# A decode kernel's last weight matrix loaded in two pieces instead of five, with seven tiny loads behind it

## The chip, the cores and the metric

The kernel runs on one core of one Trainium2 chip. The metric is device time in microseconds, the median of several executions. Beside it stands one profiled execution, with a trace of every engine and every DMA packet.

## The reference

One token (a row `x` of 1024 values, bf16) goes through an attention block with a key and value cache and, beside it, an MLP mixer; both are added to `x`. Cut to what matters here:

```python
xn = layernorm(x)
# A: 32 query heads over 4 groups of keys and values, 65536 keys of 128 values each
q = xn @ wq
p = softmax(q @ k.T * 128**-0.5);  o = p @ v;  a = o @ wo
# B: S is 1, so shifting along the sequence leaves zeros
h   = gelu(layernorm(xn) @ w1);   hs = shifted(h) @ w2;   x1 = xn + hs
b   = x1 + gelu(layernorm(x1) @ w3) @ w4          # w3: 1024 x 3584, w4: 3584 x 1024
out = x + a + b
```

With one token, `shifted(h)` is zero and `x1` is `xn`, but the kernel still loads `w1` and `w2` and multiplies by them. The caches are 64 MB for the keys and 64 MB for the values (in units of 1024 x 1024 bytes); every weight is read once. So the work is some 170 MB of reads with little arithmetic on each byte.

## The kernel before, in words

All large operands go through five buffers (`SLOTS`, line 16) of 32 KB in each of 128 partitions. A list, `items` (lines 82 to 91), gives the order in which they are loaded and used: the two halves of `wq`; then for each of four groups four times a tile of 16384 keys (K) and one of values (V), with `w3` and `w1` put in between; `wo` for the group after its tiles; at the end `w2` and the pieces of `w4`. `issue` (line 98) takes a slot and starts one DMA for one item on SP's queue (line 118). The loop at line 440 calls `ensure(i + LOOKAHEAD)`, which issues items up to four ahead, and then computes item `i`. A load waits on SP until the slot that it takes, that of the item five places before, has been read.

A K tile is transposed in place by VectorE (line 353), multiplied by the queries on TensorE (line 357), and its scores go through a maximum (line 361), an exponential on ScalarE (line 374) and a transpose (line 377); the V tile is multiplied by the result (line 389). `group_end` (line 399) joins the four tiles of a group.

The output row is accumulated in one PSUM tile, `psB`, by `row_acc` (line 159, the matmul is line 160): row 0 holds columns 0 to 511 and row 32 columns 512 to 1023, in two column groups of TensorE. A vector of one column is the stationary operand, and 512 columns of a weight row block are streamed through. `compute_wo` does 16 such matmuls for each group, `compute_w2` 16.

`w4` has 3584 rows, 28 for each partition. A "row" of a piece, in what follows, means one of these 28: 128 rows of the matrix, one in each partition, 256 KB in all, and two matmuls (columns 0 to 511 and 512 to 1023). `W4_PIECES` (line 19) says how many of them each load of `w4` has: 16, 8, 2, 1 and 1. `compute_w4(q)` (line 326) does 2 matmuls for each row of piece `q`, once that piece has landed. Its vector, `dst_h`, was made far earlier by `compute_w3`. After the last piece ScalarE copies one half of `psB` (line 336) and issues its store (line 339), and VectorE copies the other half (line 337), which SP stores (line 340).

The layout of `w4` puts the 28 rows of a partition one behind the other in memory, 2 KB each; a piece of n rows is n x 2 KB in a stretch for each partition:

```python
w4_v = B_w4.rearrange("(m c) n -> m c n", c=FC)
c0 = w4_start[item[1]]
src = w4_v[:, c0:c0 + W4_PIECES[item[1]], :].rearrange("p c n -> p (c n)")
```

Each DMA on the queues of SP and ScalarE is given one of eight semaphores in turn (they are called lanes below); a DMA that takes a lane waits until the lane's DMA before it has landed. At the end of the kernel all have to have landed.

## Time and profile before

| | |
|---|---|
| median of 3 executions | 406.71 us (406.63 to 406.77) |
| the profiled execution's own time | 406.69 us |
| its span, first to last instruction | 404.8 us |
| TensorE matmuls, busy | 245.7 us (61%) |
| VectorE, busy | 215.7 us (53%) |
| ScalarE, busy | 37.7 us (9%) |
| bytes moved by DMA | 170.11 MB, 420 GB/s over the span |
| mean granted TensorE clock | 0.796 of full |

The page of the profile gives busy times, a row of slices in time, the DMA queues, and the chain of work that ended last, followed back from the end. Lines of the timeline give start and length in microseconds, the engine (PE is TensorE, PEld its weight loads, DVE VectorE, ACT ScalarE, SPq the sequencer of SP that issues DMAs), the line of the kernel, the operation with output and inputs, and in brackets the idle time before it and what ended it. Views of stretches give the busy time of each engine in a window, the number of instructions that were at work in it, the clock that TensorE was granted, the mean share of the 16 DMA engines that was busy, and GB/s. Views of DMA issues give the size of each load and the time from issue to landing.

### The profile page before, as it was taken

The page shows a single profiled execution, that of the slowest core. Times are in us where ns is not written, and L with a number is a line of the kernel's source. Part 1 is how long each engine was busy: PE and PEld are TensorE (multiplying, and loading weights), DVE is VectorE, ACT ScalarE, POOL GpSimd, SP SyncE. Part 2 cuts the span into 40 slices and gives each one's busy share as a digit, 9 for nine tenths or more (in the row PEclk, how much of TensorE's full clock was granted, in tenths as well). Part 3 has the DMA queues.
Part 4 walks back from the last instruction along what each step waited for, and adds up shares of the span by engine and source line. Part 5 has one row for each costly group of instructions (what it writes and reads, how often), then busy time and mean ns, then how long its engine had stood idle before and what let it go on. Part 6 is the DMA issues. An engine that isn't in the chain of part 4 may idle for free.

```text
span 404.8 us, 3326 instructions
## 1 busy us (share of the span) xinstructions
PE 245.7 (61%) x1400; PEld 95.7 (24%) x1400; DVE 215.7 (53%) x235; ACT 37.7 (9%) x60; POOL 11.2 (3%) x30
## 2 busy tenths in 40 slices
PE   0385565328475847557657948384659474758456
PEld 0132222103132312112223313131233121213122
DVE  0419474017484848346665847475748383838500
ACT  0101101100201010120210010101010101010100
POOL 5001000000000000000010000000000000000000
PEclk9998878857795778768595868888958797679898
DMA  8999999999999999999999999999999999999993
GB/s 363 415 424 449 418 426 434 430 418 444 434 408 439 447 416 419 458 418 416 447 431 413 437 444 414 435 440 418 430 440 424 428 439 427 425 437 413 440 415 134
DMA packets 7065, 170.11 MB, mean 420 GB/s; under 512 B 1023, under 2 KB 1033, under 8 KB 1418
## 3 DMA queue, kind: packets, MB, share of 16 engines
q1 hardware_dynamic: 6772, 169.87, 98.0%
q8 instruction: 11, 0.18, 0.2%
q0 software_dynamic: 128, 0.02, 0.0%
q10 hardware_dynamic: 150, 0.01, 0.0%
q14 instruction: 4, 0.03, 0.0%
HBM read 169.88 MB, written 0.01 MB: 420 GB/s over the span
## 4 chain that ended last, share of the span: by engine, by line
DMA 54%; PE 23%; DVE 17%; ACT 2%; another core or an unknown queue 1%; issue 1%; DVEq 0%; ACTq 0%
DMA slot<-in_A_k_cache_dram 44%; DVE slot L353 11%; PE sc L357 10%; DMA slot<-in_B_w_dram 7%; PE psB L160 5%; PE oacc L389 4%; DMA x_bf<-in_A_x_dram 3%; DVE pT L377 2%; DVE mx L361 2%; ACT p_sb L374 2%; PE rows L244 1%; PE pm_e L417 1%; DVE m L365 0%; PE pm_mx L363 0%
## 5 line engine op out<-in xcount | busy, mean ns | idle before, releaser
L353 DVE STREAM_TRANSPOSE slot<-slot 128x2048 f32<-128x2048 f32 x64 | 142.3, 2281 | 61.1 <-DMA slot<-in_A_k_cache_dram 61.1
L357 PE MATMUL sc<-slot,qst 128*128 128x512 bf16 x512 | 131.6, 411 | 40.9 <-DVE slot L353 40.9
L389 PE MATMUL oacc<-slot,pT 128*32 128x512 bf16 x512 | 56.0, 616 | 48.0 <-DVE pT L377 48.0
L357 PEld LDWEIGHTS <-qst 128*128 128x128 bf16 x512 | 51.6, 103 | 125.1 <-issue 45.9
L361 DVE TENSOR_REDUCE mx<-sc 128x1 f32<-128x1024 f32 x16 | 19.6, 1225 | 34.7 <-PE sc L357 34.7
L374 ACT ACTIVATE p_sb<-sc,nball 128x1024 bf16<-128x1024 f32 x16 | 17.8, 1114 | 209.8 <-DVE nball L372 209.8
L389 PEld LDWEIGHTS <-pT 128*32 128x32 bf16 x512 | 17.5, 139 | 75.0 <-DVE pT L377 49.4
L377 DVE STREAM_TRANSPOSE pT<-p_sb 128x1024 bf16<-128x1024 bf16 x16 | 19.9, 1245 | 23.3 <-ACT p_sb L374 23.3
L244 PE MATMUL rows<-slot,xpad 128*32 128x512 bf16 (+1 forms) x144 | 13.6, 509 | 6.1 <-DMA slot<-in_B_w_dram 6.1
L363 PE MATMUL pm_mx<-ident_f,mx 128*1 128x128 f32 x16 | 4.3, 270 | 21.1 <-DVE mx L361 21.1
L160 PE MATMUL psB<-slot,oT 128*1 128x512 bf16 x64 | 12.6, 564 | 4.3 <-DVE oT L428 4.3
L394 ACT COPY ob<-oacc 128x512 f32<-128x512 f32 x12 | 7.0, 586 | 58.6 <-PE oacc L389 58.6
L160 PE MATMUL psB<-slot,dst_h 128*1 128x512 bf16 x56 | 7.9, 444 | 3.2 <-DMA slot<-in_B_w_dram 3.2
L370 PE MATMUL pm_mx<-ident_f,rep 1*128 1x1 f32 x16 | 3.5, 222 | 9.9 <-DVE rep L367 9.9
L417 PE MATMUL pm_e<-og,selbig 128*128 128x128 f32 x32 | 7.4, 403 | 3.4 <-DVE og L409 3.4
L244 PEld LDWEIGHTS <-xpad 128*32 128x32 bf16 x144 | 5.7, 127 | 15.0 <-issue 13.7
L172 PE MATMUL pm_ln<-ln_rowsum_a,ones_f 128*128 128x1 f32 x2 | 0.6, 348 | 13.6 <-DVE psel L229 13.6
L337 DVE CAST out<-psB 64x256 bf16<-64x256 f32 x1 | 0.4, 417 | 15.2 <-ACT out L336 15.2
L363 PEld LDWEIGHTS pm_mx<-ident_f,mx 128*1 128x1 f32 x16 | 1.3, 79 | 29.0 <-DVE mx L361 29.0
L417 PEld LDWEIGHTS pm_e<-og,selbig 128*128 128x128 f32 x32 | 6.3, 293 | 6.7 <-DVE og L409 6.7
L365 DVE TENSOR_REDUCE m<-pm_mx 1x8 f32<-1x128 f32 x16 | 4.4, 278 | 5.8 <-PE pm_mx L363 5.8
L374 ACT ACT_TABLE_LOAD x3 | 3.8, 1283 | 35.6 <-DVE nball L372 35.6
(97 smaller groups left out, 79.3 us busy)
## 6 DMA issues: line engine op xcount, KB each, us to landing
slot<-in_A_k_cache_dram SPq DMA_DIRECT2D x16, 4096.0 KB, 34.5
slot<-in_A_v_cache_dram SPq DMA_DIRECT2D x16, 4096.0 KB, 35.5
slot<-in_A_wq_dram SPq DMA_DIRECT2D x2, 4096.0 KB, 21.4
slot<-in_A_wo_dram SPq DMA_DIRECT2D x4, 2048.0 KB, 38.4
slot<-in_B_w_dram SPq DMA_DIRECT2D x2, 3584.0 KB, 42.6
slot<-in_B_w_dram SPq DMA_DIRECT2D x3, 2048.0 KB, 26.9
slot<-in_B_w_dram SPq DMA_DIRECT2D x1, 4096.0 KB, 27.8
slot<-in_B_w_dram SPq DMA_DIRECT2D x1, 512.0 KB, 16.1
```

The costliest lines, as they stand in the source:

```text
L160: nc.tensor.matmul(psB[32 * j:32 * j + 1, :], lhsT=lhsT, rhs=rhs, start=(not row_started[j]), stop=False, tile_position=(0, 32 * j), skip_ ...
L244: nc.tensor.matmul(acc[32 * j:32 * j + 32, bk, 0:width], lhsT=xp[:, c, :], rhs=wt[:, cl, ch * width:(ch + 1) * width], start=(c == 0), sto ...
L353: nc.vector.transpose(out=kf[:, cg, :], in_=kf[:, cg, :])
L357: nc.tensor.matmul(sc[:, hf, :], lhsT=qst[g % 2][:, o:o + 128], rhs=kr[:, cg, hf, :, bp // 2, :, bp % 2], start=(cg == 0 and bp == 0), sto ...
L361: nc.vector.reduce_max(out=mx[:], in_=sc[:].rearrange("p h n -> p (h n)"), axis=AX.X)
L363: nc.tensor.transpose(pm[0:1, 0:P], mx[:, 0:1], ident_f[:])
L365: nc.vector.reduce_max(out=m8[:], in_=pm[0:1, 0:P].rearrange("o (j h) -> o h j", h=8), axis=AX.X)
L374: nc.scalar.activation(out=p_sb[:], in_=sc[:], func=ACTF.Exp, bias=nball[:, r:r + 1], scale=SCALE, accum_out=lall[:, r:r + 1])
L377: nc.vector.transpose(out=pT[:], in_=p_sb[:])
L389: nc.tensor.matmul(oacc[32 * u:32 * (u + 1), :], lhsT=pT[:, hf, 32 * t:32 * (t + 1)], rhs=vt[:, :, hf, t, :], start=(hf == 0 and t < 4), s ...
L394: nc.scalar.copy(out=ob[:], in_=oacc[:])
L417: nc.tensor.matmul(pe[:, 0:P], lhsT=selbig[:, cg, :], rhs=og[:, 128 * cg:128 * (cg + 1)], start=(cg == 0), stop=(cg == 3))
```

## The change

`w4` comes in two loads, of 16 and of 12 rows, instead of five. As soon as the last load has been issued, seven loads are issued on the same queue, from the first bytes of `x` into a small tile that nothing reads: 8 bytes for each of 9, 10, 11, 12, 13, 14 and 15 partitions. They take lanes like all other loads; in the order of SP's instructions the fourth to seventh wait for the landing of the last V tile, of `wo` of the last group, of `w2` and of the first piece of `w4`, and SP's store of the output, behind them, waits for the landing of the first of them. On the other engines the instructions and their order are the same; only the waits of the `w4` matmuls are fewer. The added lines shift later line numbers: 118 becomes 119, 160 becomes 161, 340 becomes 341.

```diff
-W4_PIECES = (16, 8, 2, 1, 1)
+PROBES = (9, 10, 11, 12, 13, 14, 15)
+W4_PIECES = (16, 12)
...
+
+    probe = const.tile([16, 16, 4], BF16, name="probe")
+    xv = A_x[0, 0, :].rearrange("(p c) -> p c", c=32)
+    probed = False
     for i, it in enumerate(items):
         ensure(i + LOOKAHEAD)
+        if n_issued[0] == len(items) and not probed:
+            probed = True
+            for k in PROBES:
+                nc.sync.dma_start(out=probe[0:k, k - 1, :], in_=xv[0:k, 0:4])
         compute[it[0]](*it[1:])
```

## The prediction

> **What bounds the kernel now.** I read the page first, its slices in time and its queues. Nearly all bytes come through one queue, SP's, and the DMA engines are full in every slice but the last. (First row: DMA share in tenths over 40 slices of 10.1 us; second: packets, MB, share of the time of 16 engines.)

> ```profile
> DMA  8999999999999999999999999999999999999993
> ...
> q1 hardware_dynamic: 6772, 169.87, 98.0%
> ```

> So up to some 395 us the time is bytes over bandwidth, and the change moves no byte there. What is left to change is the last slice. I therefore read the end of the chain of waits (start us, length us):

> ```profile
> 365.42 27.79 DMA slot<-in_B_w_dram
> 393.21 0.04 issue
> 393.26 7.49 PE psB L160 x54
> 400.75 0.01 issue
> 400.76 0.40 PE psB L160 x2
> ```

> The wait for w4's first piece ends at 393.21; TensorE then works 28 rows of two matmuls with one short stop, and ends at 401.15. The copies and stores of the output end the span at 404.8. The profiled execution took 406.69 us, 1.89 more than its span, and the median of the runs is 406.71; I add differences to 406.69.

> Next the DMA issues of this stretch (KB, us from issue to landing), with issue times from SP's timeline: 374.86, 383.30 (374.86 + 8.77 - 0.33), 388.38, 390.11.

> ```profile
> slot<-in_B_w_dram SPq DMA_DIRECT2D x1, 2048.0 KB, 23.3
> slot<-in_B_w_dram SPq DMA_DIRECT2D x1, 512.0 KB, 16.1
> slot<-in_B_w_dram SPq DMA_DIRECT2D x1, 256.0 KB, 11.7
> ...
> slot<-in_B_w_dram SPq DMA_DIRECT2D x1, 256.0 KB, 10.6
> ```

> Issue plus landing time gives the arrivals of w4's pieces: 16 rows 393.22, 8 rows 398.16, 2 rows 399.40, 1 row 400.08, 1 row 400.71. The early arrivals of small pieces are what the kernel lives from: when the last byte lands, one row is left to multiply.

> What a row costs is in TensorE's timeline (start, length, then the weight loads, which go with the rows):

> ```profile
> 386.45 1.89 PE L160 MATMUL psB<-slot,oT 128*1 128x512 bf16 x16 [1.06 <-DVE oT L428]
> ...
> 395.34 0.13 PEld L160 LDWEIGHTS <-dst_h 128*1 128x1 bf16 x2 [0.29 <-issue]
> 395.77 0.13 PEld L160 LDWEIGHTS <-dst_h 128*1 128x1 bf16 x2 [0.29 <-issue]
> ```

> At full granted clock 16 matmuls are 8 rows in 1.89 us; the last matmul lasts 0.38 (median 379 ns at this line), so a row takes (1.89 - 0.38)/7 = 0.2155 us. At half clock rows start 0.427 us apart (395.34, 395.77), and a matmul lasts 0.63 (the longest at this line).

> **The change, part by part.** *Three loads go (2, 1 and 1 rows); the 8-row load becomes one of 12.* Bytes are the same. Nothing starves by that: the queue holds the 4 MB piece and more when the 12-row load is issued at 374.86, so only the order of issue changes. The 12-row piece has landed when all its 3 MB have: 398.16 plus 1 MB. In before that MB took 2.55 us (400.71 - 398.16) in small packets; in big ones 2 MB took 4.94 (398.16 - 393.22), so 2.47 a MB. The packet view shows at most more: from 366 to 390 us 10.21 MB at 99.5% of 16 engines, 26.7 KB per engine-us; from 396.5 to 400.4 us 0.65 MB at 44.4%, 23.5; by that ratio 2.55 becomes 2.24. I take 400.63, with bounds 400.40 and 400.71.

> *TensorE's last 12 rows move behind that landing.* In before, 11 of them ran beside the arrivals from 398.2 on; that cover goes. Start 400.63 + 0.04 = 400.67. At full clock 11 x 0.2155 + 0.38 = 2.75, so TensorE ends at 403.42 instead of 401.15: **+2.27**. Everything after (ScalarE's and VectorE's copies, two stores) follows unchanged.

> *The clock of these 12 rows.* The gap before them is new: the 16 rows of the first piece end near 398.37 (393.26 + 8 rows at 0.427 less 0.19 for the first and eighth step, + 8 at 0.2155 + 0.165), so TensorE stands still for 2.3 us; where those rows run at full clock it is 3.8 us (from 396.87). The granted clock changes in this trace only on a grid of 3.41 us. One call for such stretches (stretch, length, TensorE busy us, ..., granted clock, DMA share, GB/s):

> ```profile
> 188.12:191.53 3.41, 1.51 (x7) 0.46 (x5) 1.72 (x3) 0.00 (x0) 0.00 (x0) 1.00 0.96 413
> 191.53:194.94 3.41, 0.26 (x1) 0.18 (x1) 0.47 (x2) 2.49 (x3) 0.00 (x0) 0.50 0.94 404
> 280.28:283.69 3.41, 1.65 (x11) 0.74 (x8) 3.41 (x2) 0.59 (x1) 0.00 (x0) 1.00 0.96 413
> 283.69:287.10 3.41, 2.82 (x13) 1.07 (x12) 3.41 (x3) 0.00 (x0) 0.00 (x0) 1.00 0.98 416
> 297.34:300.76 3.42, 2.56 (x25) 0.85 (x18) 1.34 (x2) 0.00 (x0) 0.00 (x0) 0.50 0.99 422
> 300.76:304.17 3.41, 2.34 (x12) 2.04 (x14) 0.94 (x4) 0.00 (x0) 0.00 (x0) 0.50 0.96 413
> 379.26:382.68 3.42, 2.60 (x28) 0.99 (x32) 2.67 (x6) 0.00 (x0) 0.00 (x0) 0.50 1.13 484
> 382.68:386.09 3.41, 1.85 (x22) 1.27 (x14) 1.41 (x4) 0.00 (x0) 0.00 (x0) 1.00 0.98 423
> ```

> The reader is to see two thresholds. From full clock, 1.51 of 3.41 us busy (44%) is followed by half and 1.65 (48%) by full. From half clock, 2.56 (75%) stays half and 2.60 (76%) rises. Half clock thus lasts at least one whole stretch, in which 3.41/0.427 = 8 rows pass, at 8 x (0.427 - 0.2155) = 1.69 more than at full clock. Which of three ends comes depends on where the grid lies:
> - *All full.* On the grid of this execution the stretch 396.33 to 399.74 is busy for 2.04 us (60%), so the next one is full, to 403.16: +2.27.
> - *One half stretch.* Grid 1.09 later (397.42, 400.84, 404.25): busy 1.14 before the gap and 0.17 behind it is 38%, so half clock from 400.84; 8 rows pass until 404.25, the rest at full: +2.27 + 1.69 = **+3.96**. Where the half stretch reaches past the tail it is less, down to about +3.4.
> - *All half.* Grid 0.13 earlier, where the first piece runs at full clock and ends at 396.87: 396.20 to 399.61 is busy 20%, so half from 399.61; the next stretch is busy 2.35 of 3.41 (69%, below 75%), so it stays half: 400.67 + 11 x 0.427 + 0.63 = 406.00: +4.85.

> Working the two thresholds through the tail at 25 equally spaced positions of the grid, with the landings above, gives about 3 times the first, 15 times the second and 7 times the third. Nothing in one profile shows whether the grid lies alike in every execution; the 0.14 us spread of before says nothing, as its end hangs on the landing at 400.71 and not on the clock.

> [...]

> *The seven probes.* In the order of SP's instructions in the changed program they follow the last w4 load. Each issue is 0.33 us (the rows of SP's timeline), 7 x 0.33 = 2.3 us, less three removed; SP is idle from 390.4 to 402.0 in before. The fourth to seventh wait for the landings of the last V, wo, w2 and w4's first piece, the latest at 393.22; behind them stands only SP's output store, ready at 402.02 in before and later now. That store also waits for the landing of the first probe, which is queued right behind the 12 rows. Bounds: nothing, or a small load's 6.9 us (dst_g, 2 KB) counted from 400.63: 407.5, which is 1.6 past the store's new time of 405.98 (402.02 + 3.96). The nearest row is w4's last piece, also small and queued behind others: it landed 0.63 after its neighbour, so 401.3 for the probe, well in time. I take nothing. The last probe, issued at 393.3, would at the 12.3 us of x_bf land at 405.6, before the end of the span in any case.

> [...]

> **The rivals.**
> - *All full clock*, 406.69 + 2.27 = 408.96. For it: the grid of the one profile. Against: few grids.
> - *All half*, 406.69 + 4.85 = 411.54. For it: 7 of 25 positions.
> - *Not slower*: the engines' shares after 396.5 us (0.63 over 2.5 us, 0.10 over 2.2 us) show that engines finish one by one. If one big load let them end together, the last landing would be 396.5 + 1.58 + 0.22 = 398.3, as the first piece's rows end; 398.35 + 2.75 = 401.10, so 406.65. From a landing of 398.3 down the change costs nothing, and above 399.2 it costs over 0.2% (0.81 us, about what a measurement can tell from no change). Against: the 8 rows alone landed at 398.16 with 1 MB to come, and nothing moves bytes between engines.
> - *The probes hold the end* (or a load of nine to fifteen partitions is slow in a way no row shows): 410.65 + 1.6 = 412.25.

> **How the numbers follow.** One half stretch 0.52 (410.65, own range 410.0 to 410.8), all full 0.20, all half 0.18, probes 0.06, not slower 0.04 (half of it faster, half the same). Forecast 410.65. The range takes in all full with the early landing (408.73) up to all half with the late one (411.62): 408.7 to 411.7, 0.90 of the chance; without its lower end it would hold 0.70. Slower 0.96, same 0.02, faster 0.02.

> **What would show it.** The 12-row load lands at 400.4 to 400.7; TensorE waits there once, for a w4 DMA, and starts 24 matmuls right after; its end is 2.75 us later with clock 1.00, 4.4 with one half stretch, 5.3 with all half. The clock's grid lies elsewhere than here. Times of single runs differ by more than the 0.14 us of before, if the grid is free. Wrong would be: a landing before 399.2, a first probe that lands after the output copies, or a half clock that a gap of 2.3 us doesn't bring.

## The result, and the profile after

The changed kernel took 409.45 us (median of 3 executions, 409.40 to 410.89), before 406.71. The ratio is 1.0081, with a 95% interval of 1.0059 to 1.0103: slower by 0.8%. The profiled execution took 409.45 us with a span of 407.7.

The page of the changed kernel, slices and queue as they were shown of before. (DMA share in tenths; SP's queue with packets, MB, share of 16 engines.)

```profile
DMA  8999999999999999999999999999999999999990
...
q1 hardware_dynamic: 6508, 169.87, 97.2%
```

The same bytes in 264 packets fewer, and the last slice, a 3 in before, is now a 0: the loads are over, and TensorE still works. The end of its chain of waits (start us, length us, what):

```profile
372.36 1.91 PE sc L358 x8
374.27 0.02 issue
374.28 25.61 DMA slot<-in_B_w_dram
399.89 0.04 issue
399.94 4.33 PE psB L161 x24
404.26 0.02 issue
404.29 0.37 ACT out L337
```

In before the last landing, at 400.71, was followed by 2 matmuls. Here the last landing comes at 399.89 and is followed by 24, that is by all 12 rows. The timeline of TensorE says how they went (start, length, then weight loads, which go with the rows):

```profile
392.65 3.62 PE L161 MATMUL psB<-slot,dst_h 128*1 128x512 bf16 x32 [1.28 <-DMA slot<-in_B_w_dram]
399.94 4.30 PE L161 MATMUL psB<-slot,dst_h 128*1 128x512 bf16 x24 [3.67 <-DMA slot<-in_B_w_dram]
...
400.74 0.13 PEld L161 LDWEIGHTS <-dst_h 128*1 128x1 bf16 x2 [0.29 <-issue]
401.17 0.13 PEld L161 LDWEIGHTS <-dst_h 128*1 128x1 bf16 x2 [0.30 <-issue]
```

The 16 rows ran at full clock (3.62 us, rows 0.2155 apart). The 12 rows start 3.67 us later, at first 0.43 apart (400.74, 401.17): half clock. The view of stretches, on this execution's grid of 3.41 us (stretch, length, TensorE busy us, ..., granted clock, DMA share, GB/s):

```profile
382.63:386.05 3.42, 1.58 (x18) 1.19 (x10) 1.65 (x5) 0.00 (x0) 0.00 (x0) 1.00 1.00 431
386.05:389.46 3.41, 3.32 (x16) 0.99 (x18) 0.03 (x1) 0.00 (x0) 0.00 (x0) 0.50 0.98 420
...
396.29:399.70 3.41, 0.00 (x0) 0.00 (x0) 0.00 (x0) 0.00 (x0) 0.00 (x0) 1.00 0.29 106
399.70:403.11 3.41, 3.17 (x16) 1.00 (x17) 0.00 (x0) 0.00 (x0) 0.00 (x0) 0.50 0.00 0
403.11:406.53 3.42, 1.13 (x10) 0.26 (x6) 0.42 (x1) 0.37 (x1) 0.00 (x0) 1.00 0.00 1
```

The new gap filled the stretch before 399.70 (busy 0.00), the next stretch had half clock, and the rows that were left then ran at full. The first two lines show the same thing earlier: a stretch busy for 1.58 of 3.41 us (46%) was followed by half.

### The profile page after: what moved, and what is told of

Read it like the earlier page. It is cut to its first block, busy times and chain, and to the rows that moved or that the text cites. A ratio compares the mean times of both kernels' runs of the same rounds, so it can differ in the third digit from the quotient of the medians.

```text
span 407.7 us, 3328 instructions
## 1 busy us (share of the span) xinstructions
PE 244.4 (60%) x1400; PEld 94.3 (23%) x1400; DVE 215.7 (53%) x235; ACT 37.7 (9%) x60; POOL 11.2 (3%) x30
## 2 busy tenths in 40 slices
DMA packets 6801, 170.11 MB, mean 417 GB/s; under 512 B 1143, under 2 KB 1153, under 8 KB 1154
## 3 DMA queue, kind: packets, MB, share of 16 engines
q1 hardware_dynamic: 6508, 169.87, 97.2%
## 4 chain that ended last, share of the span: by engine, by line
DMA 61%; PE 18%; DVE 16%; ACT 2%; another core or an unknown queue 1%; issue 1%; DVEq 0%; ACTq 0%
DMA slot<-in_A_k_cache_dram 52%; DVE slot L354 11%; PE sc L358 11%; DMA slot<-in_B_w_dram 6%; DMA x_bf<-in_A_x_dram 3%; PE oacc L390 2%; PE psB L161 2%; PE rows L245 1%; DVE pT L378 1%; DVE mx L362 1%; ACT p_sb L375 1%; ACT L184 0%; DVE m L366 0%; PE pm_e L418 0%
## 5 line engine op out<-in xcount | busy, mean ns | idle before, releaser
L378 DVE STREAM_TRANSPOSE pT<-p_sb 128x1024 bf16<-128x1024 bf16 x16 | 19.9, 1245 | 23.3 <-ACT p_sb L375 23.3
L418 PE MATMUL pm_e<-og,selbig 128*128 128x128 f32 x32 | 6.5, 364 | 3.4 <-DVE og L410 3.4
## 6 DMA issues: line engine op xcount, KB each, us to landing
slot<-in_A_wo_dram SPq DMA_DIRECT2D x4, 2048.0 KB
slot<-in_B_w_dram SPq DMA_DIRECT2D x2, 2048.0 KB
```

Source lines behind the costliest of these rows:

```text
L378: nc.vector.transpose(out=pT[:], in_=p_sb[:])
L418: nc.tensor.matmul(pe[:, 0:P], lhsT=selbig[:, cg, :], rhs=og[:, 128 * cg:128 * (cg + 1)], start=(cg == 0), stop=(cg == 3))
```

## The experiments

Each kernel was timed in turn with before on one chip; where a time of before is given here, it is the one measured beside the kernel. Experiments 9 to 12 come from what the first eight left open. The edits of 1 to 7 are shown against the changed kernel, those of 9 to 12 against before.

**1. The tiny loads taken away** (label e1_no_probes).

```diff
-PROBES = (9, 10, 11, 12, 13, 14, 15)
+PROBES = ()
```

> The two big pieces without the seven tiny loads. Theory (the 12 rows of work behind the last landing, part of them at half clock, are the whole cost): as the changed kernel, 409.4 to 410.9, with single runs that differ by over 1 us. Rival (the tiny loads hold the output store or the end): back to about 406.7, or at least 1.5 below the changed kernel.

Measured: 409.49 (six executions: 407.99, 409.16, 409.33, 409.64, 409.69, 410.57), before 406.57, ratio 1.0068 (1.0054 to 1.0083). The tiny loads are not the cost. The six times lie in three places, one near 408.0, four from 409.2 to 409.7, one at 410.6; the changed kernel's three lie at the second and third. The profiled execution was the first, and its chain and stretches show why it was quick:

```profile
374.12 25.89 DMA slot<-in_B_w_dram
400.01 0.04 issue
400.05 2.77 PE psB L161 x24
```

```profile
394.94:398.35 3.41, 1.43 (x14) 0.49 (x11) 0.00 (x0) 0.00 (x0) 0.00 (x0) 1.00 0.62 257
398.35:401.77 3.42, 1.72 (x16) 0.70 (x17) 0.00 (x0) 0.00 (x0) 0.00 (x0) 1.00 0.05 22
```

The same gap of 3.7 us and the same landing (400.01 beside 399.89), but the grid lies 2.1 us later, the gap is shared by two stretches that are busy 42% and 50%, and both are followed by full clock. The 12 rows take 2.77 us instead of 4.33. That 42% is below the 44% after which, in before's trace, the clock fell; the lower threshold is not as sharp as the prediction had it.

**2. The tiny loads alone, behind the old five pieces** (label e2_probes_only).

```diff
-W4_PIECES = (16, 12)
+W4_PIECES = (16, 8, 2, 1, 1)
```

> The old five pieces with the seven tiny loads behind them. Theory: 406.7, within 0.2 us of before, since the last tiny load lands about 1.3 us behind the last piece and the output store comes later than that. Rival (the tiny loads cost): 408 to 409.5.

Measured: 406.12 (405.92 to 406.44), before 406.57, ratio 0.9989 (0.9981 to 0.9998). The tiny loads don't cost, but neither theory had it 0.45 us faster. Experiments 8 to 11 come back to that.

**3. TensorE kept at work in the gap** (label e3_busy_gap).

```diff
+        if q == 0:
+            junk = ps_M.tile([P, 512], F32, name="pm_junk", tag="pm")
+            for cl in range(10):
+                for j in range(2):
+                    nc.tensor.matmul(junk[32 * j:32 * j + 1, :], lhsT=st["hT"][:, cl:cl + 1],
+                                     rhs=wt[:, cl, 512 * j:512 * (j + 1)], start=True, stop=True,
+                                     tile_position=(0, 32 * j), skip_group_check=True)
         if q == len(W4_PIECES) - 1:
```

> The changed kernel with 20 more matmuls (ten rows' worth, into a tile that nothing reads) between the 16 rows and the 12, so that TensorE works through most of the gap. Theory (half clock in the tail costs 1.5 to 1.7 us of the change): all 12 rows at full granted clock, 2.75 us from landing to end instead of 4.3, so 407.9, and single runs within 0.4 us of one another. Rival (the rows cost the same whatever stands before them): 409.4 or more.

Measured: 408.01 (407.94 to 408.08), before 406.57, ratio 1.0035 (1.0023 to 1.0047). More work, less time: 1.5 us below experiment 1, and the spread of 2.6 us is gone (0.14). TensorE's timeline, with the added matmuls at line 338:

```profile
392.81 3.62 PE L161 MATMUL psB<-slot,dst_h 128*1 128x512 bf16 x32 [1.50 <-DMA slot<-in_B_w_dram]
396.26 2.33 PE L338 MATMUL pm_junk<-slot,dst_h 128*1 128x512 bf16 x20
400.11 2.75 PE L161 MATMUL psB<-slot,dst_h 128*1 128x512 bf16 x24 [1.53 <-DMA slot<-in_B_w_dram]
```

The 12 rows take 2.75 us, as worked out for full clock. So of the changed kernel's cost half clock is 1.5 us in the median.

**4. One row of the 12 multiplied** (label e5_one_row); 11 rows of `w4` are left out of the product.

```diff
-        for cl in range(n):
+        for cl in range(n if q == 0 else 1):
```

> The changed kernel with only one of the 12 rows multiplied (11 rows of w4 are left out of the product, the loads are the same). It times the landing of the big piece by itself. Theory (fewer and bigger packets save 0.1 to 0.3 us, the rest of the 0.82 us by which the profiled landing was earlier is chance): 406.4 to 406.6. Rival (the big piece itself lands 0.8 us earlier): 405.9. Second rival (a landing that is late in most runs): above 406.8.

Measured: 405.76 (405.45 to 406.08), before 406.57, ratio 0.9978 (0.9969 to 0.9987). The big piece landed at 400.05, so the first rival had the number right: the landing is earlier than before's as a rule (0.5 to 0.7 us here), not by chance. Its cause is another matter: experiment 9 gives most of it to where the buffers lie. With the clock as granted, the work of 11 rows is worth 409.49 - 405.76 = 3.7 us.

**5. Four rows last** (label e4_last_four), without tiny loads.

```diff
-W4_PIECES = (16, 12)
+W4_PIECES = (16, 8, 4)
```

> Pieces of 16, 8 and 4 rows, no tiny loads: four rows instead of 12 behind the last landing, and no gap of more than about 1 us before them. Theory: from the landing to TensorE's end 0.04 + 3 x 0.2155 + 0.38 = 1.07 us at full clock, against 0.44 in before; with packets a little bigger 407.0 to 407.2, single runs within 0.6 us of one another. Rival (a wait before the last piece brings half clock whatever its length): 4 rows at half clock, 1.95 us, so 408.

Measured: 406.61 (406.48 to 406.92), before 406.57, ratio 1.0002 (0.9993 to 1.0011). The time is 0.4 us below the lower end of what was expected. The tail itself is as worked out (landing 400.03, the 8 matmuls 1.03 us at full clock, gap 0.55 us), but it starts 0.5 to 0.7 us earlier than in the two profiles of before (400.54 and 400.71), which hides it. Behind this gap of 0.55 us the clock stayed full.

**6. Seventy tiny loads** (label e6_seventy).

```diff
-PROBES = (9, 10, 11, 12, 13, 14, 15)
+PROBES = (9, 10, 11, 12, 13, 14, 15) * 10
```

> The changed kernel with ten times its tiny loads, 70 instead of 7. The profiled changed kernel shows their landings 0.2 us apart behind the big piece. Theory (that spacing is a cost of each tiny load, hidden only as long as they are few): the last of 70 lands about 14 us after the big piece, at 414, and the end with it: 415 to 417. Rival (the cost is the packets' own 9 ns, and the spacing is something else): 409.4 to 410.9 as with seven.

Measured: 429.92 (2 executions), before 406.57. Both expectations missed. SP's timeline shows the price, and SP's waits from 374 to 430 us (total, times, longest) tell what it is:

```profile
400.25 25.32 SPq L450 DMA_DIRECT2D probe<-in_A_x_dram  x63
425.62 0.60 SPq L341 DMA_DIRECT2D out_dram<-out  x1
...
SPq L450 <- DMA probe<-in_A_x_dram: 7.0, 1, 7.0
SPq L450 <- DMA out_dram<-out: 0.9, 1, 0.9
```

The eighth tiny load waits until the first has landed, behind the big piece; that is the one long wait, 7.0 us, and it ends at 400.2. Then SP issues the other 63 in 25.32 us, 0.40 each, and on the way waits only once, for 0.9 us. So the price is SP's own time for issuing a load (the prediction had 0.33 us for each), not a wait for lanes. The last tiny load of experiment 2 landed 1.4 us after its issue, so with eight lanes, as an estimate, the waits alone would let one go every 0.2 us. The output store stands behind all of them on SP. With seven there is no such queue: in the changed kernel SP issued the last of them at 392.6 and waited for the first to land until 400.0, 5.1 us before the store was due.

**7. The pieces of 2 and 1 rows as one of 3** (label e7_four_pieces), without tiny loads.

```diff
-W4_PIECES = (16, 12)
+W4_PIECES = (16, 8, 3, 1)
```

> Pieces of 16, 8, 3 and 1 rows, no tiny loads: as before, but the pieces of 2 and 1 rows are one. TensorE ends the 8 rows 0.7 us before the last landing and the 3 rows just at it, so one row is left, as in before. Theory: the landing decides, one load fewer saves less than 0.1 us: 406.4 to 406.6 beside a before of 406.57. Rival (the last landing of before is late by itself, by the 0.5 us that the kernels of the first set show): 406.0 to 406.2.

Measured: 406.17 (405.91 to 406.34), before 406.57, ratio 0.9989 (0.9980 to 0.9998). Again 0.4 below before, with nearly before's pieces.

**8. Before once more** (label r_before), unchanged.

> The kernel before, unchanged, profiled once more. In the first set the old pieces with tiny loads ran at 406.12 and before at 406.57, and w4's first landing was 0.4 to 0.7 us earlier in the five profiles after the first. Theory (the earlier landings come with other programs, not with the tiny loads or the sizes): first w4 landing at 393.1 to 393.3 again, 406.6. Rival (the one profile of before was a late one by chance): 392.6, and a time as its other runs.

Measured: 406.54, first `w4` landing 393.02, last 400.54. Before's landings are no accident; in the eight other kernels so far they were 0.2 to 0.7 us earlier from the first `w4` piece on, ahead of any byte that the change concerns. What those kernels share is the small tile `probe`, which I had left allocated even where nothing was loaded into it. In the compiled programs it moves what is allocated behind it, the five big buffers among it, by 128 bytes per partition: they begin at byte 37856 of a partition in before and at 37984 in the changed kernel.

**9. That tile alone** (label f1_pad128), in before.

```diff
+    pad = const.tile([P, 64], BF16, name="pad")
     for i, it in enumerate(items):
```

> The kernel before with a tile of 128 bytes per partition that nothing uses, allocated where the changed kernel has its small tile; it moves the five big buffers 128 bytes up (37856 to 37984 bytes from the partition's start). Theory (the 0.4 us by which the first set's kernels had w4 earlier come from where the buffers lie): 406.15, first w4 landing near 392.6. Rival (they come from something else in those programs): 406.55.

Measured: 406.09 (405.96 to 406.63), before 406.51, ratio 0.9990 (0.9981 to 0.9999). A tile that nothing touches gives the 0.4 us, as in experiments 2 and 7. Experiments 2 and 9 differ by 0.03 us, less than their runs scatter, so no cost of the seven tiny loads can be told from none. In the profile, of an execution of 406.23, `w4` landed first at 392.93, later than the 392.6 that was expected and 0.1 to 0.3 earlier than in before.

**10. 32 bytes instead** (label f2_pad32): the buffers begin at 37888, 148 times 256.

```diff
+    pad = const.tile([P, 16], BF16, name="pad")
     for i, it in enumerate(items):
```

> The kernel before with 32 bytes put there instead, so that the buffers begin at 37888, a multiple of 512. Theory (what counts is the place in a block of 256 or 512 bytes): at least as early as with 128 bytes, 406.0 to 406.15. Rival (any move does it, or none): the same time as with 128 bytes, whichever that is.

Measured: 404.55 (404.42 to 404.79), before 406.51, ratio 0.9951 (0.9939 to 0.9962). This beats before and the changed kernel, by more than either expectation had. The stream itself is faster; the packet views of the stretch from 100 to 300 us, in which the loads never stop, for before, for the 128 bytes and for the 32 bytes:

```profile
DMA packets 3302, 86.06 MB, mean 430 GB/s; under 512 B 414, under 2 KB 416, under 8 KB 416
```

```profile
DMA packets 3303, 86.10 MB, mean 430 GB/s; under 512 B 414, under 2 KB 416, under 8 KB 416
```

```profile
DMA packets 3312, 86.39 MB, mean 432 GB/s; under 512 B 414, under 2 KB 416, under 8 KB 416
```

A packet is 0.03 MB, and before profiled again has 86.00, so this view tells the 32 bytes from the rest but not the 128 bytes from none. The records of the packets do. A packet of 32 KB took on average, from 60 to 350 us, 1219.5 and 1219.9 ns in the two profiles of before, 1218.8 with the 128 bytes and 1214.4 with the 32 bytes; the changed kernel has 1218.7. As an estimate, each of the 16 engines handles some 324 such packets (170.11 MB), so 5.1 ns a packet make 1.7 of the 2.0 us, and 0.7 to 1.1 ns make 0.2 to 0.4 of the 0.4 us. VectorE's transposes in the same buffers last 2.28 us in all of these kernels, so it is not the compute on the buffers that changed.

**11. Two pieces and nothing else** (label f3_two_pieces_only), before with `W4_PIECES = (16, 12)`, buffers where before has them.

```diff
-W4_PIECES = (16, 8, 2, 1, 1)
+W4_PIECES = (16, 12)
```

> The kernel before with pieces of 16 and 12 rows and nothing else: no tiny loads and no small tile, so the buffers lie as in before. Theory: the two pieces cost 2.5 to 4.5 us in single runs by where the clock's grid lies, and the place of the buffers takes back 0.4 in the changed kernel; so 409.8 here, single runs over 1 us apart. Rival (the small tile's 128 bytes do nothing): 409.4 as the changed kernel.

Measured: 409.88 (408.52, 409.70, 409.77, 409.99, 410.05, 410.89), before 406.51, ratio 1.0080 (1.0066 to 1.0093). This is the cost of the pieces with nothing given back: +3.4, beside +2.7 to +2.9 with the small tile. The profiled execution has the short gap of the prediction's main case (16 rows partly at half clock, 2.01 us idle):

```profile
394.38:397.79 3.41, 3.41 (x20) 1.09 (x18) 0.00 (x0) 0.00 (x0) 0.00 (x0) 0.50 0.84 358
397.79:401.21 3.42, 1.41 (x14) 0.50 (x12) 0.00 (x0) 0.00 (x0) 0.00 (x0) 1.00 0.11 43
401.21:404.62 3.41, 3.41 (x18) 0.95 (x14) 0.00 (x0) 0.00 (x0) 0.00 (x0) 0.50 0.00 0
```

A stretch that is busy for 1.41 of 3.41 us (41%), with a gap far shorter than itself, was followed by half clock.

**12. 288 bytes** (label f4_pad288): the buffers begin at 38144, 149 times 256, no multiple of 512.

```diff
+    pad = const.tile([P, 144], BF16, name="pad")
     for i, it in enumerate(items):
```

> The kernel before with 288 bytes put there, so that the big buffers begin at 38144, a multiple of 256 and not of 512. Theory (blocks of 256 bytes are what counts): 404.55 as with 32 bytes. Rival (blocks of 512 bytes, or the first multiple only by chance): 406.1 or more.

Measured: 404.52 (404.39 to 404.70), before 406.54, ratio 0.9950 (0.9937 to 0.9964). The start at 149 times 256 gives the same time as that at 148 times 256 (404.55), so the gain doesn't hang on a multiple of 512. The packet view from 100 to 300 us:

```profile
DMA packets 3316, 86.52 MB, mean 433 GB/s; under 512 B 414, under 2 KB 416, under 8 KB 416
```

A packet of 32 KB took 1214.4 ns again.

## Why the prediction was right, and where it was not

The sign, the mechanism and the range held: 12 rows wait for the last landing, alone, and part of them run at half clock. The likeliest case was put at 410.65, 1.20 too high. In the profiled execution the terms are these.

- **Landing of the last piece: 400.63 said, 399.89 measured, -0.74.** This is the term that was mis-sized, outside its own bounds (400.40 to 400.71). The part of it that I argued, big packets, was roughly right: from the first piece's landing the last 3 MB took 7.28 us (392.61 to 399.89) beside 7.50 in before, so -0.22 where I took -0.08; experiment 11, which has nothing but the two pieces, shows 7.31, and before profiled again 7.52. The rest was there before: the first piece landed 0.60 earlier, some 0.4 of it from the place of the buffers (by the times of experiment 9), 0.2 within what two profiles of before differ by (393.21 and 393.02). I had taken the small tile for nothing but a target of tiny loads.
- **The 12 rows: landing to TensorE's end 4.48 said, 4.37 measured.** At full clock 2.79 was said; experiment 1's profile has 2.81 and experiment 3's 2.82.
- **From TensorE's end to the time: 5.54 in before, 5.19 after, -0.35.** The prediction had everything after the rows unchanged. Of it some 0.2 lies between TensorE's end and the span's end (3.65 and 3.44, with spans to 0.1 us); all profiled kernels with two pieces show 3.37 to 3.44 there, the others 3.62 to 3.74, but for the seventy loads, whose store is held up. What makes it, the runs don't tell.
- **Half clock: +1.69 said, +1.5 in the median** (409.49 in experiment 1 less 408.01 in experiment 3). The three cases appear as three groups of times in experiments 1 and 11 together: 2, 8 and 2 of 12 executions, where 25 positions of the grid had given 3, 15 and 7. Two of the groups are each tied to a profile; the highest is put to the all-half case by its time alone. Right in kind, wrong in two details. On this execution's grid, 0.04 us from that of before, I had all rows at full clock. `wo`'s rows had run at half clock here (46% busy in the stretch before). So they ended later, `w2`'s rows fell into the next stretch and kept it busy, the 16 rows ran at full clock where in before they had begun at half, and the gap became a whole idle stretch. So the position of the grid alone doesn't decide. The other detail is the lower threshold, which is taken up below the list.
- **Whether the grid is free** was open. The grids of the profiled executions, counted from the span's start, lie from 0.02 to 3.02 us past a multiple of 3.41, and those of before's two profiles are 2.6 us apart; it is free. With TensorE kept at work the two-piece kernel's scatter went from 2.6 to 0.14 us (experiment 3), so it comes from the clock of the 12 rows; before scatters by 0.6.
- **The probes: nothing said, and nothing that can be told from the scatter measured** (experiments 2 and 9).
- **Not slower**: it needed a landing of 398.3; the landings of the big piece were 399.89 to 400.33. The traces have 16 landing records for each of these loads: those of the changed kernel's big piece lie from 396.56 to 399.89, over 3.33 us, and those of the last load in before from 397.35 to 400.71, over 3.36 us, so one big load didn't let its parts end together. It was rightly small.

Before's trace put the lower threshold between 44 and 48% of a stretch, and other profiles don't bear that out. After full clock, a stretch busy for 42% was followed by full in experiment 1, and one busy for 52% by half in experiment 5:

```profile
382.32:385.73 3.41, 1.78 (x22) 1.19 (x10) 1.46 (x4) 0.00 (x0) 0.00 (x0) 1.00 0.96 413
385.73:389.14 3.41, 3.11 (x16) 1.00 (x18) 0.23 (x1) 0.00 (x0) 0.00 (x0) 0.50 0.95 408
```

So from about 41% to over 50% the busy share alone doesn't tell what follows, and what else decides stays open; the counts of 3, 15 and 7 rest on a threshold that isn't sharp. The upper one is sharper: in all fourteen profiles stretches up to 77% stayed at half, and those from 76% rose.

## What to carry to other kernels

When a load-bound kernel ends on a matrix product, the work that is left after the last landing is the cost; size the last pieces so that one piece's work fits into the next one's transfer, and no more than that: a last piece of 4 rows cost 0.4 us here beside one of 1 row (experiments 5 and 7, buffers in the same place), and one of 12 rows 3.4 (experiment 11). A gap that such a piece opens can cost a second time through TensorE's clock (1.5 us in the median here), by a grid that lay anywhere from 0.02 to 3.02 us past a multiple of 3.41 in the profiles, so a time that scatters by microseconds from run to run is a reason to look at the stretches before the last work. Before crediting or blaming an edit for a few tenths of a per cent, look at what it moved in memory: an unused tile changed this kernel by 0.1 to 0.5%.

## What the runs showed of the hardware that I had not expected

Beside the start at a multiple of 256, the starts 96 and 224 bytes past one cost 0.4% and 0.5% in time, and 0.36% and 0.42% for a packet: most of the loss comes with the first 96 bytes. What makes it, the runs don't show.

TensorE's clock could be kept full by matmuls that nobody needs: behind ten rows of them the 12 rows took 2.75 us instead of 4.30, and the changed kernel was 1.5 us faster in the median (experiment 3). Loads of a few bytes cost SP's time for issuing them: seven, issued while the big pieces were under way, cost nothing that can be measured, and of seventy 63 could go out only behind the last landing, 0.40 us each, and made the kernel 20 us slower.
